# Attention feeding an MLP on one core: three hand-assigned two-bank accumulators, five score jobs at three points, all masks on VectorE, w_out queued ahead of the casts

## The chip, the cores and the metric

One core of one Trainium2 chip. The metric is device time in microseconds (us). A quoted median is over all executions of a kernel in a set of runs; the profile shows one execution, with a *span* a little under its time. Engines: PE is TensorE (matmuls and transposes; PEld are its weight loads), DVE is VectorE, ACT is ScalarE, POOL is GpSimd.

## The reference

Batch 8, 8 heads, 576 positions, 64 dimensions per head. Four heads see a local window of 32 positions, four see every 32nd position. The attention output, 4608 tokens of 512, goes through an MLP with the Mish activation. All inputs and the output are float32.

```python
rel = pos[:, None] - pos[None, :]
mask_local = (rel >= 0) & (rel < 32)
mask_strided = (rel >= 0) & (pos[None, :] % 32 == pos[:, None] % 32)
# heads 0-3 local, heads 4-7 strided; softmax over the allowed positions
attn_out = softmax(where(mask, q @ k.T / 8, -1e9)) @ v
x = attn_out.transpose(0, 2, 1, 3).reshape(4608, 512)
h = x @ w_in                               # 512 -> 2048
out = (h * tanh(softplus(h))) @ w_out      # 2048 -> 512
```

## The kernel before

The MLP runs in nine blocks of 512 tokens. MLP1 of a block is 8 groups of eight matmuls; MLP2 is 16 groups of four. Attention of the next batch is woven in: q and k are transposed between the groups of MLP1, and scores, P times V and the transposes of the result stand between the groups of MLP2. I call P times V of strided tile i "V(s,i)" and of local tile i "V(l,i)". A block takes the time that PE takes for its queue, plus every wait in it.

PSUM is full: three two-bank accumulators (two for the MLP, one for scores) and two one-bank tiles with the tag `pt`. P times V **and** all transposes share these two.

```python
ps_mm = ctx.enter_context(tc.tile_pool(name="psmm", bufs=2, space=PS))
ps_s = ctx.enter_context(tc.tile_pool(name="pss", bufs=1, space=PS))
ps_t = ctx.enter_context(tc.tile_pool(name="pst", bufs=2, space=PS))
...
def tile_t(name):
    return ps_t.tile([128, 512], F32, tag="pt", name=name)
...
def qk(self, kind, i, meng, from_mm=False):      # scores of one job
    ps = tile_s(from_mm)
    ...  # matmuls that contract over 64 rows, half of the array each
    nc.scalar.activation(pt[0:n, :, 0:nw], ps[0:n, :, 0:nw], AF.Exp, scale=scale)
    if meng is not None:
        self.mask(kind, i, meng)                 # P *= mask, on engine meng
...
def pv(self, kind, i):                           # V(kind, i)
    po = tile_t("po")[:, 0:4 * (D + 1)].rearrange("p (h d) -> p h d", h=4)
    self.pv_mm(kind, i, po)
    nc.vector.reciprocal(rden[0:m, :], po[0:m, :, D])       # the normalisation:
    nc.vector.tensor_tensor(...)                            # frees the pt tile
```

Six score jobs per batch, each at its own place in MLP2, four of them masked by GpSimd. Entry i of the list follows group i of MLP2:

```python
Po, Dv = nc.gpsimd, nc.vector
return [
    [Q("s", 0, Dv)], [], [Q("s", 1, Dv)],
    [Q("s", 2, Po), V("s", 0)],
    [Q("l", 0, Po), V("s", 1)],
    [Q("l", 1, Po), V("s", 2), V("s", 3)],
    [Q("l", 2, Po), V("s", 4)], [V("s", 5), V("s", 6)],
    [V("s", 7), V("l", 0)], [V("l", 1)], [X("s", 0), V("l", 2)],
    [X("s", 1), V("l", 3)], [X("l", 0), V("l", 4)], [V("l", 5)],
    [X("l", 1)], [],
]
```

The order of the loads and GpSimd's casts around block 0, where v of batch 1 is first needed:

```python
load_qk_str(1)
load_w_out(0, 2)           # first half of w_out, GpSimd's DMA queue
...
load_v(1)                  # another queue
...
cast_qk_loc(1, Po, Po)
cast_v(1, Po, Po)          # GpSimd waits here until v has landed
load_w_out(2, 4)           # so these are issued only afterwards
load_qk_str(2)
```

The softmax here doesn't subtract the row's maximum and nothing guards it: scores larger than these inputs give would overflow.

Of the kernel before, what the change touches and what calls it, by code (L numbers as in the profile page):

```python
# [16 lines left out]
NW = 6  # L17
WQ = 96
# [19 lines left out]
def kernel(ctx, tc, q, k, v, moe_w_in, moe_w_out, out):  # L38
# [33 lines left out]
    P_s = [const.tile([PN, 2, 6 * PN + 56], BF16, name=f"Ps{i}") for i in range(3)]  # L72
    P_l = [const.tile([128, 2, 4 * WQ + 32], BF16, name=f"Pl{i}") for i in range(3)]
# [9 lines left out]
    ps_mm = ctx.enter_context(tc.tile_pool(name="psmm", bufs=2, space=PS))  # L83
    ps_s = ctx.enter_context(tc.tile_pool(name="pss", bufs=1, space=PS))
    ps_t = ctx.enter_context(tc.tile_pool(name="pst", bufs=2, space=PS))

    def tile_s(from_mm=False):
        if from_mm:
            return ps_mm.tile([128, 2, 512], F32, tag="mm", name="ps")
        return ps_s.tile([128, 2, 512], F32, tag="ps", name="ps")  # L90
# [124 lines left out]
    S_JOBS = [S_UNITS[0:6], S_UNITS[6:12], S_UNITS[12:16]]  # L215
    S_AT = {u: (i, n) for i, job in enumerate(S_JOBS) for n, u in enumerate(job)}

    class Attn:
# [3 lines left out]
        def qk(self, kind, i, meng, from_mm=False):  # L222
            ps = tile_s(from_mm)
            if kind == "l":
                nu, n, w, pt, mk = 4, 128, WQ, P_l[i], loc
                for u in range(nu):
                    hp, c0 = u // 2, WQ * (2 * i + u % 2)
                    for e in range(2):
                        nc.tensor.matmul(  # L229
                            ps[:, e, WQ * u:WQ * u + WQ],  # L230
                            lhsT=kTl[64 * e:64 * e + 64, hp, c0:c0 + 128],
                            rhs=qTl[64 * e:64 * e + 64, hp, c0:c0 + WQ],
                            start=True, stop=True,
                        )
            else:
                nu, n, w, pt, mk = len(S_JOBS[i]), PN, PN, P_s[i], stm
                for u, (jj, h) in enumerate(S_JOBS[i]):
                    c0 = PN * (4 * h + jj)
                    for e in range(2):
                        nc.tensor.matmul(  # L240
                            ps[:, e, PN * u:PN * u + PN],
                            lhsT=kTs[64 * e:64 * e + 64, c0:c0 + 128],
                            rhs=qTs[64 * e:64 * e + 64, c0:c0 + PN],
                            start=True, stop=True,
                        )
            nw = nu * w
            nc.scalar.activation(pt[0:n, :, 0:nw], ps[0:n, :, 0:nw], AF.Exp, scale=scale)  # L247
            if meng is not None:
                self.mask(kind, i, meng)

        def mask(self, kind, i, meng):
            nu, n, w, pt, mk = (
                (4, 128, WQ, P_l[i], loc) if kind == "l" else (len(S_JOBS[i]), PN, PN, P_s[i], stm)
            )
# [7 lines left out]
        def pv_mm(self, kind, i, po):  # L262
            for h in range(4):
                if kind == "l":
                    n, rhs = 128, vl[self.b % 2][:, i, h, :]
                    pt, c0 = P_l[i // 2][:, h % 2], WQ * (2 * (h // 2) + i % 2)
                else:
                    n, rhs = PN, vs[self.b % 2][0:PN, h, i, :]
                    job, u = S_AT[i // 2, h]
                    pt, c0 = P_s[job][:, i % 2], PN * u  # L270
# [17 lines left out]
        def pv2(self, kind, i, from_mm=False):  # L288

            po = tile_s(from_mm)[:, :, 0:4 * (D + 1)].rearrange("p e (h d) -> p e h d", h=4)  # L290
# [38 lines left out]
    def attn_steps(b):  # L329
        a = Attn(b)  # L330
        Po, Dv = nc.gpsimd, nc.vector
# [71 lines left out]
    with tc.manual_schedule():  # L403
# [43 lines left out]
        for i in range(3):  # L447
            a.qk("s", i, None, i > 0)
# [108 lines left out]
```

## Time and profile before

| | before |
|---|---|
| median (range), first three runs | 341.93 us (340.81 to 342.24) |
| span of the profiled execution, mean PE clock | 339.5 us, 0.999 |
| MLP2 of block 0 | 23.11 us (43.11 to 66.22) |
| blocks 1 to 6 (of that, MLP2) | 35.4 to 35.6 us (about 19.5) |

The prediction shows the lines of the page, of the stretches and of PE's timeline. In a line of a timeline the columns are start, length, engine, source line, operation, tiles, shape and number of instructions; a bracket gives the idle time of the engine just before and what ended it. Two rows of the page's list of costly groups are added here. They are P times V, and the columns after the bar are busy us, mean ns of one, idle us of PE just before them in the whole run, and what ended most of it:

```profile
L271 PE MATMUL po<-vs,Ps 72*128 72x65 bf16 x224 | 14.2, 195 | 2.3 <-POOL Ps L256 2.3
...
L271 PE MATMUL po<-vl,Pl 128*128 128x65 bf16 x176 | 12.9, 196 | 2.8 <-DVE rden L282 1.5
```

In 339.5 us PE stands only 5.1 us in front of P times V, and 2.3 of these are the one wait for GpSimd in block 0.

The table of stretches (from:to, length, busy us of PE, PEld, DVE, ACT, POOL, clock, DMA share, GB/s) gives MLP2 of block 0 as

```profile
43.11:66.22 23.11, 19.72 (x221) 10.77 (x223) 11.21 (x34) 10.41 (x13) 14.52 (x14) 1.00 0.82 140
```

### The profile page before, as it was taken

The numbers are of one execution on the slowest core, as the hardware profiler recorded it, in microseconds if no ns is written. First come the engines' busy times: TensorE is split into PE (matmuls) and PEld (weight loads), VectorE is DVE, ScalarE is ACT, GpSimd is POOL, SyncE is SP. The second block draws the span as 40 slices with busy tenths as digits, with TensorE's granted clock in tenths as the row PEclk, the third lists the DMA queues.
The fourth block names the chain that finished last, engine by engine and source line by source line (L and its number), as shares of the span: only waits on it lengthen the run. The fifth ranks groups of instructions, "written<-read, shape, count | busy, mean of one in ns | idle before, by whom it ended". The sixth has DMA issues, their size and how long they took to land.

```text
span 339.5 us, 6425 instructions
## 1 busy us (share of the span) xinstructions
PE 313.8 (92%) x2761; PEld 171.1 (50%) x2808; DVE 114.3 (34%) x306; ACT 176.2 (52%) x194; POOL 111.0 (33%) x105
## 2 busy tenths in 40 slices
PE   2669996999999999999999999999999999999994
PEld 1554553554455545554579555544554454444441
DVE  4670345323552346134622362236323640000000
ACT  3574562556637563747464646564566537414511
POOL 4354049334681049102921094008500700000000
PEclk9999999999999999999999999999999999999999
DMA  6999958999947911595149712941010011011011
GB/s 178 217 220 205 212 95 128 215 200 284 193 110 209 188 37 64 159 198 79 63 116 202 120 62 64 229 74 60 17 51 0 2 64 62 2 62 62 0 57 68
DMA packets 49596, 39.29 MB, mean 116 GB/s; under 512 B 27168, under 2 KB 42080, under 8 KB 49568
## 3 DMA queue, kind: packets, MB, share of 16 engines
q1 hardware_dynamic: 38272, 29.88, 38.6%
q0 software_dynamic: 11152, 8.92, 16.9%
q8 instruction: 22, 0.36, 0.5%
q10 hardware_dynamic: 144, 0.08, 0.1%
q14 instruction: 6, 0.05, 0.1%
HBM read 38.34 MB, written 9.44 MB: 141 GB/s over the span
## 4 chain that ended last, share of the span: by engine, by line
PE 73%; DMA 12%; DVE 4%; POOL 3%; issue 3%; ACT 3%; SPq 1%; POOLq 0%; ACTq 0%
PE psh L368 32%; PE pso L388 28%; DMA vl<-in_v_dram 7%; DMA qs<-in_q_dram 4%; PE po L271 4%; PE tr L174 2%; PE tr L183 2%; ACT Ps L247 2%; DVE x_s L283 1%; PE ps L229 1%; DVE qTl L146 1%; PE ps L240 1%; PE trx L320 1%; PE trx L310 1%; POOL vl L146 1%
## 5 line engine op out<-in xcount | busy, mean ns | idle before, releaser
L388 PE MATMUL pso<-w_out,gT 128*128 128x512 bf16 x546 | 137.3, 379 | 1.6 <-issue 0.2
L368 PE MATMUL psh<-xT,w_in 128*128 128x512 bf16 (+1 forms) x623 | 133.1, 359 | 1.3 <-ACT gT L373 0.2
L373 ACT ACTIVATE gT<-psh 128x1024 bf16<-128x1024 f32 x72 | 73.6, 1024 | 55.7 <-PE psh L368 55.6
L368 PEld LDWEIGHTS <-w_in 128*128 128x128 bf16 x640 | 60.1, 98 | 54.6 <-issue 2.2
L388 PEld LDWEIGHTS <-gT 128*128 128x128 bf16 x576 | 49.0, 97 | 44.3
L144 ACT COPY xT<-trx 128x576 bf16<-128x576 bf16 x32 | 20.3, 639 | 44.1 <-PE trx L320 28.0
L256 POOL TENSOR_TENSOR Ps<-Ps,consts_sb 72x576 bf16<-72x576 bf16 x7 | 8.9, 1273 | 88.8 <-ACT Ps L247 88.7
L256 POOL TENSOR_TENSOR Pl<-Pl,consts_sb 128x768 bf16<-128x768 bf16 x21 | 33.8, 1638 | 1.6 <-ACT Pl L247 1.6
L395 ACT COPY osb<-pso 128x1024 f32<-128x1024 f32 x18 | 18.2, 1012 | 27.4 <-PE pso L388 27.4
L282 DVE RECIPROCAL rden<-po 72x4 f32<-72x4 f32 (+1 forms) x100 | 17.7, 177 | 35.3 <-PE po L271 35.3
L247 ACT ACTIVATE Pl<-ps 128x768 bf16<-128x768 f32 x24 | 19.5, 811 | 14.6 <-PE ps L229 14.4
L283 DVE TENSOR_TENSOR x_s<-po,rden 72x256 bf16<-72x256 f32 x56 | 23.6, 421 | 1.9
L247 ACT ACTIVATE Ps<-ps 72x864 bf16<-72x864 f32 (+1 forms) x24 | 19.1, 806 | 9.5 <-PE ps L240 9.4
L146 DVE COPY kTl<-tr 128x576 bf16<-128x576 bf16 x14 | 10.6, 758 | 30.2 <-PE tr L183 30.2
L146 POOL CAST vs<-vs 72x2048 bf16<-72x2048 f32 x7 | 13.3, 1896 | 18.3 <-DMA vs<-in_v_dram 18.3
L283 DVE TENSOR_TENSOR x_l<-po,rden 96x256 bf16<-96x256 f32 x44 | 18.5, 420 | 1.5
L256 DVE TENSOR_TENSOR Ps<-Ps,consts_sb 72x864 bf16<-72x864 bf16 (+1 forms) x17 | 10.3, 605 | 22.0 <-ACT Ps L247 22.0
L146 DVE COPY kTs<-tr 128x576 bf16<-128x576 bf16 x14 | 6.4, 458 | 30.7 <-PE tr L174 30.7
L271 PEld LDWEIGHTS <-Ps 72*128 72x128 bf16 x256 | 12.1, 102 | 8.8 <-POOL Ps L256 2.4
L271 PE MATMUL po<-vs,Ps 72*128 72x65 bf16 x224 | 14.2, 195 | 2.3 <-POOL Ps L256 2.3
L146 DVE COPY qTl<-tr 128x576 bf16<-128x576 bf16 x14 | 10.6, 756 | 14.8 <-PE tr L183 14.8
L271 PE MATMUL po<-vl,Pl 128*128 128x65 bf16 x176 | 12.9, 196 | 2.8 <-DVE rden L282 1.5
(61 smaller groups left out, 227.0 us busy)
## 6 DMA issues: line engine op xcount, KB each, us to landing
out_dram<-osb SPq DMA_DIRECT2D x18, 512.0 KB, 3.5
vl<-in_v_dram SPq DMA_DIRECT2D x7, 768.0 KB, 17.2
vs<-in_v_dram SPq DMA_DIRECT2D x8, 576.0 KB
kl<-in_k_dram SPq DMA_DIRECT2D x7, 576.0 KB
ql<-in_q_dram SPq DMA_DIRECT2D x7, 576.0 KB, 9.6
w_out<-in_moe_w_out_dram POOLq DMA_DIRECT2D x4, 512.0 KB, 12.5
ks<-in_k_dram POOLq DMA_DIRECT2D x7, 288.0 KB, 12.4
qs<-in_q_dram POOLq DMA_DIRECT2D x7, 288.0 KB, 13.8
```

The costliest lines, as they stand in the source:

```text
L144: nc.scalar.copy(out_, in_)
L146: eng.tensor_copy(out_, in_)
L174: nc.tensor.transpose(tr[:, PN * u:PN * u + PN], src[0:PN, h, 128 * jj:128 * jj + 128], ident[0:PN, 0:PN],)
L247: nc.scalar.activation(pt[0:n, :, 0:nw], ps[0:n, :, 0:nw], AF.Exp, scale=scale)
L256: meng.tensor_tensor(out=pm, in0=pm, in1=mk[0:n, :].unsqueeze(1).unsqueeze(1).to_broadcast([n, 2, nu, w]), op=ALU.mult,)
L271: nc.tensor.matmul(po[:, h, :], lhsT=pt[0:n, c0:c0 + 128], rhs=rhs, start=True, stop=True,)
L282: nc.vector.reciprocal(rden[0:m, :], po[0:m, :, D])
L283: nc.vector.tensor_tensor(out=dst.rearrange("p (h d) -> p h d", h=4), in0=po[0:m, :, 0:D], in1=rden[0:m, :].unsqueeze(2).to_broadcast([m, ...
L368: nc.tensor.matmul(ps[:, u, o:o + n], lhsT=w_in[:, cc, fc * 128:(fc + 1) * 128], rhs=xT[:, cc, a:a + n], start=(cc == 2), stop=(cc == 1),)
L373: nc.scalar.activation(gT[:, 2 * g:2 * g + 2, :], ps[:], AF.Mish)
L388: nc.tensor.matmul(p[:, ot % 2, :], lhsT=gT[:, fc, 128 * ot:128 * ot + 128], rhs=w_out[:, fc, :], start=(fc == 0), stop=(fc == 15),)
L395: nc.scalar.copy(osb[:], p[:])
```

## The change

Its intent: fewer switches of PE between the scores' half-array matmuls and everything else, no wait for a single score accumulator, no slow GpSimd masks, and w_out in time. There are five score jobs at three points of MLP2, each point using accumulators that the MLP leaves free just then; all masks move to VectorE; the second half of w_out and the q/k loads of batch 2 are issued before GpSimd waits for v.

```diff
-    ps_mm = ctx.enter_context(tc.tile_pool(name="psmm", bufs=2, space=PS))
-    ps_s = ctx.enter_context(tc.tile_pool(name="pss", bufs=1, space=PS))
+    ps_a = ctx.enter_context(tc.tile_pool(name="psa", bufs=1, space=PS))
+    def acc(i, name):
+        return ps_a.tile([128, 2, 512], F32, tag=f"acc{i}", name=name)
 ...
+    L_UNITS = [(i, hp) for i in range(NW) for hp in range(2)]
+    PARTS = {
+        "s": [S_UNITS[0:6], S_UNITS[6:12], S_UNITS[12:16]],
+        "l": [L_UNITS[0:5], L_UNITS[5:10], L_UNITS[10:12]],
+    }
 ...
-    def attn_steps(b):
+    def attn_steps(b, x, y):
-        Po, Dv = nc.gpsimd, nc.vector
+        Q = lambda i_acc, *parts: (lambda: a.qk(parts, i_acc, nc.vector))
+        at = [
+            [], [], [],
+            [V("s", 0)], [V("s", 1)], [V("s", 2)], [V("s", 3)], [V("s", 4)],
+            [V("s", 5), V("l", 5)], [V("s", 6), V("l", 0)], [V("s", 7), V("l", 1)],
+            [X("s", 0), V("l", 2)], [X("s", 1), V("l", 3)], [V("l", 4), X("l", 0)], [X("l", 1)], [],
+        ]
+        s0, s1, sl2, l0, l1 = ...
+        if x == y:       # block 0, one accumulator
+            where = {0: [(x, s0)], 2: [(x, s1)], 4: [(x, sl2)], 6: [(x, l0)], 8: [(x, l1)]}
+        else:
+            where = {1: [(x, s0), (y, s1)], 4: [(x, sl2), (y, l0)], 7: [(x, l1)]}
+        for i, jobs in where.items():
+            at[i] = [Q(i_acc, *parts) for i_acc, parts in jobs] + at[i]
 ...
-        load_w_out(0, 2)
+        load_w_out(0, 4)
 ...
         cast_qk_loc(1, Po, Po)
+        load_qk_str(2)
         cast_v(1, Po, Po)
-        load_w_out(2, 4)
-        load_qk_str(2)
```

More of the change, by code (lines that the diff above doesn't have):

```diff
@@ L71 @@
     kTs = const.tile([128, 4 * 4 * PN + 64], BF16, name="kTs")
-    P_s = [const.tile([PN, 2, 6 * PN + 56], BF16, name=f"Ps{i}") for i in range(3)]
-    P_l = [const.tile([128, 2, 4 * WQ + 32], BF16, name=f"Pl{i}") for i in range(3)]
+    P_s = [const.tile([PN, 2, n * PN + 56], BF16, name=f"Ps{i}") for i, n in enumerate((6, 6, 4))]
+    P_l = [const.tile([128, 2, n * WQ + 32], BF16, name=f"Pl{i}") for i, n in enumerate((5, 5, 2))]
     gate = const.tile([1, 256], BF16, name="gate")
@@ L82 @@
     PS = bass.MemoryType.PSUM
-    ps_mm = ctx.enter_context(tc.tile_pool(name="psmm", bufs=2, space=PS))
-    ps_s = ctx.enter_context(tc.tile_pool(name="pss", bufs=1, space=PS))
+    ps_a = ctx.enter_context(tc.tile_pool(name="psa", bufs=1, space=PS))
     ps_t = ctx.enter_context(tc.tile_pool(name="pst", bufs=2, space=PS))
-    def tile_s(from_mm=False):
-        if from_mm:
-            return ps_mm.tile([128, 2, 512], F32, tag="mm", name="ps")
-        return ps_s.tile([128, 2, 512], F32, tag="ps", name="ps")
+    def acc(i, name):
+        return ps_a.tile([128, 2, 512], F32, tag=f"acc{i}", name=name)
     def tile_t(name):
@@ L214 @@
     S_UNITS = [(jj, h) for jj in range(4) for h in range(4)]
-    S_JOBS = [S_UNITS[0:6], S_UNITS[6:12], S_UNITS[12:16]]
-    S_AT = {u: (i, n) for i, job in enumerate(S_JOBS) for n, u in enumerate(job)}
+    L_UNITS = [(i, hp) for i in range(NW) for hp in range(2)]
[3 more added lines that the diff above has]
+    }
+    AT = {kd: {u: (i, n) for i, p in enumerate(PARTS[kd]) for n, u in enumerate(p)} for kd in "sl"}
     class Attn:
@@ L220, in __init__ @@
             self.b = b
-        def qk(self, kind, i, meng, from_mm=False):
-            ps = tile_s(from_mm)
-            if kind == "l":
-                nu, n, w, pt, mk = 4, 128, WQ, P_l[i], loc
-                for u in range(nu):
-                    hp, c0 = u // 2, WQ * (2 * i + u % 2)
-                    for e in range(2):
-                        nc.tensor.matmul(
-                            ps[:, e, WQ * u:WQ * u + WQ],
-                            lhsT=kTl[64 * e:64 * e + 64, hp, c0:c0 + 128],
-                            rhs=qTl[64 * e:64 * e + 64, hp, c0:c0 + WQ],
-                            start=True, stop=True,
-                        )
-            else:
-                nu, n, w, pt, mk = len(S_JOBS[i]), PN, PN, P_s[i], stm
-                for u, (jj, h) in enumerate(S_JOBS[i]):
-                    c0 = PN * (4 * h + jj)
-                    for e in range(2):
-                        nc.tensor.matmul(
-                            ps[:, e, PN * u:PN * u + PN],
-                            lhsT=kTs[64 * e:64 * e + 64, c0:c0 + 128],
-                            rhs=qTs[64 * e:64 * e + 64, c0:c0 + PN],
-                            start=True, stop=True,
-                        )
-            nw = nu * w
-            nc.scalar.activation(pt[0:n, :, 0:nw], ps[0:n, :, 0:nw], AF.Exp, scale=scale)
-            if meng is not None:
-                self.mask(kind, i, meng)
@@ new lines, in qk @@
+        def qk(self, parts, i_acc, meng=None):
+            ps, o = acc(i_acc, "ps"), 0
+            todo = []
+            for kind, i in parts:
+                w = WQ if kind == "l" else PN
+                o0 = o
+                for x, y in PARTS[kind][i]:
+                    for e in range(2):
+                        r = slice(64 * e, 64 * e + 64)
+                        if kind == "l":
+                            lhsT, rhs = kTl[r, y, WQ * x:WQ * x + 128], qTl[r, y, WQ * x:WQ * x + WQ]
+                        else:
+                            c0 = PN * (4 * y + x)
+                            lhsT, rhs = kTs[r, c0:c0 + 128], qTs[r, c0:c0 + PN]
+                        nc.tensor.matmul(ps[:, e, o:o + w], lhsT=lhsT, rhs=rhs, start=True, stop=True)
+                    o += w
+                todo.append((kind, i, o0, o - o0))
+            for kind, i, o0, nw in todo:
+                n, pt = (128, P_l[i]) if kind == "l" else (PN, P_s[i])
+                nc.scalar.activation(pt[0:n, :, 0:nw], ps[0:n, :, o0:o0 + nw], AF.Exp, scale=scale)
+                if meng is not None:
+                    self.mask(kind, i, meng)
@@ L251, in mask @@
         def mask(self, kind, i, meng):
-            nu, n, w, pt, mk = (
-                (4, 128, WQ, P_l[i], loc) if kind == "l" else (len(S_JOBS[i]), PN, PN, P_s[i], stm)
-            )
+            nu = len(PARTS[kind][i])
+            n, w, pt, mk = (128, WQ, P_l[i], loc) if kind == "l" else (PN, PN, P_s[i], stm)
             pm = pt[0:n, :, 0:nu * w].rearrange("p e (u c) -> p e u c", u=nu)
@@ L265, in pv_mm @@
                     n, rhs = 128, vl[self.b % 2][:, i, h, :]
-                    pt, c0 = P_l[i // 2][:, h % 2], WQ * (2 * (h // 2) + i % 2)
+                    part, u = AT["l"][i, h // 2]
+                    pt, c0 = P_l[part][:, h % 2], WQ * u
                 else:
                     n, rhs = PN, vs[self.b % 2][0:PN, h, i, :]
-                    job, u = S_AT[i // 2, h]
-                    pt, c0 = P_s[job][:, i % 2], PN * u
+                    part, u = AT["s"][i // 2, h]
+                    pt, c0 = P_s[part][:, i % 2], PN * u
                 nc.tensor.matmul(
@@ L286, in pv, with pv2 @@
             )
-        def pv2(self, kind, i, from_mm=False):
-            po = tile_s(from_mm)[:, :, 0:4 * (D + 1)].rearrange("p e (h d) -> p e h d", h=4)
+        def pv2(self, kind, i, i_acc):
+            po = acc(i_acc, "po2")[:, :, 0:4 * (D + 1)].rearrange("p e (h d) -> p e h d", h=4)
             m = WQ if kind == "l" else PN
@@ L327, in xt @@
                 )
-    def attn_steps(b):
+    def attn_steps(b, x, y):
         a = Attn(b)
-        Po, Dv = nc.gpsimd, nc.vector
-        Q = lambda kd, i, e: (lambda: a.qk(kd, i, e))
+        Q = lambda i_acc, *parts: (lambda: a.qk(parts, i_acc, nc.vector))
         V = lambda kd, i: (lambda: a.pv(kd, i))
         X = lambda kd, hf: (lambda: a.xt(kd, hf))
-        return [
-            [Q("s", 0, Dv)], [], [Q("s", 1, Dv)],
-            [Q("s", 2, Po), V("s", 0)],
-            [Q("l", 0, Po), V("s", 1)],
-            [Q("l", 1, Po), V("s", 2), V("s", 3)],
-            [Q("l", 2, Po), V("s", 4)], [V("s", 5), V("s", 6)],
-            [V("s", 7), V("l", 0)], [V("l", 1)], [X("s", 0), V("l", 2)],
-            [X("s", 1), V("l", 3)], [X("l", 0), V("l", 4)], [V("l", 5)],
-            [X("l", 1)], [],
-        ]
+        at = [
[3 more added lines that the diff above has]
+            [X("s", 0), V("l", 2)], [X("s", 1), V("l", 3)], [V("l", 4), X("l", 0)], [X("l", 1)], [],
+        ]
+        s0, s1, sl2, l0, l1 = (("s", 0),), (("s", 1),), (("s", 2), ("l", 2)), (("l", 0),), (("l", 1),)
+        if x == y:
+            where = {0: [(x, s0)], 2: [(x, s1)], 4: [(x, sl2)], 6: [(x, l0)], 8: [(x, l1)]}
+        else:
+            where = {1: [(x, s0), (y, s1)], 4: [(x, sl2), (y, l0)], 7: [(x, l1)]}
+        for i, jobs in where.items():
+            at[i] = [Q(i_acc, *parts) for i_acc, parts in jobs] + at[i]
+        return at
     def segs(t):
@@ L353, in segs, with mlp1 @@
         return r
-    def mlp1(t):
+    def mlp1(t, accs):
         gT = g_pool.tile([128, 16, 512], BF16, tag="gT", name="gT")
@@ L361, in group @@
             if g not in held:
-                held[g] = ps_mm.tile([128, 2, 512], F32, tag="mm", name="psh")
+                held[g] = acc(accs[g % 3], "psh")
             ps = held[g]
@@ L378, in mlp1, with mlp2 @@
         return gT, [lambda g=g: group(g) for g in range(8)]
-    def mlp2(t, gT, fc_major=False):
+    def mlp2(t, gT, accs, fc_major=False):
         po = {}
@@ L384, in group @@
             if ot // 2 not in po:
-                po[ot // 2] = ps_mm.tile([128, 2, 512], F32, tag="mm", name="pso")
+                po[ot // 2] = acc(accs[ot // 2], "pso")
             p = po[ot // 2]
@@ L447 @@
         for i in range(3):
-            a.qk("s", i, None, i > 0)
+            a.qk([("s", i)], i)
         a.mask("s", 0, Dv)
@@ L460 @@
             t_step_loc0(kl0, kTl[:, hp, 32:32 + S], hp, Sc)
-        a.pv2("s", 0)
+        a.pv2("s", 0, 0)
         a.mask("s", 2, Dv)
-        a.pv2("s", 2, True)
+        a.pv2("s", 2, 1)
         for hp in range(2):
             t_step_loc0(ql0, qTl[:, hp, :], hp, Sc)
-        a.qk("l", 0, None, True)
-        a.pv2("s", 4)
-        a.qk("l", 1, None, True)
+        a.qk([("l", 0)], 2)
+        a.pv2("s", 4, 0)
+        a.qk([("l", 1)], 1)
         a.mask("l", 0, Dv)
-        a.pv2("s", 6)
+        a.pv2("s", 6, 0)
         cast_v_loc(0, Sc, 3, 6)
-        a.qk("l", 2, None, True)
+        a.qk([("l", 2)], 2)
         a.mask("l", 1, Dv)
         load_qk_str(1)
-        load_w_out(0, 2)
+        load_w_out(0, 4)
         nc.sync.dma_start(gate[:], qs[1][0:1, 0, 0:256])
         load_v(1)
-        gT, g1 = mlp1(0)
+        accs = (2, 1, 0)
+        gT, g1 = mlp1(0, accs)
         a.xt("s", 0)
@@ L481 @@
         Sc.preload_act_table(AF.Mish)
-        a.pv2("l", 0, True)
+        a.pv2("l", 0, 1)
         a.mask("l", 2, Dv)
-        a.pv2("l", 2)
+        a.pv2("l", 2, 0)
         a.pv("l", 4)
@@ L499 @@
         for t in range(NBLK):
+            x, y, z = accs
             if t > 0:
-                gT, g1 = mlp1(t)
-            ts = t_steps(t + 1) if t + 1 < B else []
-            at = attn_steps(t + 1) if t + 1 < B else []
+                gT, g1 = mlp1(t, accs)
+            ts, at = [], []
             if t == 0:
+                ts, at = t_steps(1), attn_steps(1, y, y)
                 at[8].append(load_next)
                 at[0] = ts[2:4] + at[0] + [lambda: load_qk_str(3)]
+                out_accs, accs = (z, x), (y, z, x)
+            else:
+                if t + 1 < B:
+                    ts, at = t_steps(t + 1), attn_steps(t + 1, x, y)
+                out_accs, accs = (z, y), (z, x, y)
             for i, g in enumerate(g1):
@@ L515 @@
                 load_qk_str(t + 3)
-            for i, g in enumerate(mlp2(t, gT, fc_major=(t == 0))):
+            for i, g in enumerate(mlp2(t, gT, out_accs, fc_major=(t == 0))):
                 g()
```

## The prediction

> **What bounds the kernel now.** I read the page's busy shares first, then the table of stretches, then TensorE's timeline in one block, and then the same microseconds on the engines that feed it. The page:
>
> ```profile
> PE 313.8 (92%) x2761; PEld 171.1 (50%) x2808; DVE 114.3 (34%) x306; ACT 176.2 (52%) x194; POOL 111.0 (33%) x105
> ```
>
> TensorE (PE) is the bound on average. By stretches (columns: from:to, length, then busy us of PE, PEld, DVE, ACT, POOL, then clock, DMA share, GB/s):
>
> ```profile
> 58.60:102.00 43.40, 42.66 (x395) 22.68 (x400) 17.80 (x51) 23.76 (x27) 23.54 (x20) 1.00 1.03 200
> 137.40:172.80 35.40, 34.61 (x320) 18.38 (x325) 14.12 (x38) 20.19 (x22) 14.04 (x12) 1.00 0.60 120
> 307.00:334.80 27.80, 27.55 (x126) 12.37 (x127) 0.00 (x0) 10.22 (x11) 0.00 (x0) 1.00 0.10 38
> ```
>
> A block (512 tokens, MLP1 then MLP2) with the attention of the next batch woven in takes 35.4 us; the last two, without attention, take 27.8. Blocks 1 to 6 are alike, block 0 has a start of its own. So the change must be judged by what TensorE waits for in such a block. Its timeline around the scores of a batch (start, length, instructions; a group of four MLP2 matmuls is L388, the scores L240 and L229, P times V L271):
>
> ```profile
> 153.11 1.03 PE L388 MATMUL pso<-w_out,gT 128*128 128x512 bf16 x4
> 154.08 0.37 PE L240 MATMUL ps<-qTs,kTs 64*128 64x72 bf16 x12
> 154.38 1.68 PE L388 MATMUL pso<-w_out,gT 128*128 128x512 bf16 x7
> 156.33 0.37 PE L240 MATMUL ps<-qTs,kTs 64*128 64x72 bf16 x12 [0.27 <-ACT Ps L247]
> 156.64 1.04 PE L388 MATMUL pso<-w_out,gT 128*128 128x512 bf16 x4
> ...
> 163.39 1.03 PE L388 MATMUL pso<-w_out,gT 128*128 128x512 bf16 x4
> 164.26 0.29 PE L271 MATMUL po<-vs,Ps 72*128 72x65 bf16 x4
> 164.79 0.29 PE L271 MATMUL po<-vl,Pl 128*128 128x65 bf16 x4 [0.25 <-DVE rden L282]
> 164.92 1.02 PE L388 MATMUL pso<-w_out,gT 128*128 128x512 bf16 x4
> ```
>
> A group occupies 4 x 0.216 = 0.86 us (eight MLP1 matmuls take 1.73 on the chain that ended last). The reader is to see two kinds of loss: about 0.11 us before each score job (153.11 + 0.86 = 153.97, scores at 154.08) and 0.12 after it, six times a batch; and two real waits, one for the single score accumulator (0.12 us beyond the usual 0.11) and one of 0.25 for a small PSUM buffer that VectorE (DVE) had not emptied. Feeding engines:
>
> ```profile
> 158.08 0.65 ACT L247 ACTIVATE Ps<-ps 72x576 bf16<-72x576 f32 x1 [0.45 <-PE ps L240]
> 159.46 0.81 ACT L247 ACTIVATE Pl<-ps 128x768 bf16<-128x768 f32 x1 [0.73 <-PE ps L229]
> 163.39 1.01 ACT L395 COPY osb<-pso 128x1024 f32<-128x1024 f32 x1 [0.26 <-PE pso L388]
> ```
>
> ```profile
> 157.66 0.60 DVE L256 TENSOR_TENSOR Ps<-Ps,consts_sb 72x864 bf16<-72x864 bf16 x1 [0.74 <-ACT Ps L247]
> 158.25 0.18 DVE L282 RECIPROCAL rden<-po 72x4 f32<-72x4 f32 x1
> 158.46 0.42 DVE L283 TENSOR_TENSOR x_s<-po,rden 72x256 bf16<-72x256 f32 x1
> ```
>
> One normalisation on DVE (reciprocal and multiply) is 0.63 us. In block 0 alone GpSimd (POOL) holds PE up:
>
> ```profile
> 56.76 0.29 PE L271 MATMUL po<-vs,Ps 72*128 72x65 bf16 x4 [2.27 <-POOL Ps L256]
> ```
>
> **What the Trainium skill says.** (1) "TensorEngine Tiling (Array Packing)", Key Properties: "Mode switching requires drain". The scores contract over 64 rows, all else uses the whole array; the 0.11 + 0.12 us at each score job agree. (2) "TensorE: Matmul & The Clock Gate", Architectural detail: ScalarE and VectorE queues are strict FIFO; only weight loads are pulled ahead on TensorE. The timelines agree so far as they show: no DVE instruction is out of program order. My prediction rests on this. (3) "PSUM — Partial Sum Buffer", Specifications: 8 banks of 512 fp32. Three two-bank accumulators plus two one-bank tiles fill all eight, before and after: P times V and the transposes still share only two small tiles. (4) "SBUF — State Buffer", Who interferes with whom: a VectorE instruction with two SBUF inputs contends with GpSimd reads. In block 0 a mask took 0.76 instead of 0.60 us beside a POOL cast, so this is small.
>
> **The change part by part.**
> *Fewer switches.* Blocks 1 to 6 have three score points instead of six. Matmul work is equal. 3 x 0.23 = 0.69 us saved per block. With scores in alternating accumulators the 0.12 us wait goes too.
> *Masks on DVE.* POOL loses 1.27 + 4.83 = 6.1 us per batch, none of it on the path in blocks 1 to 6. DVE gains four masks: 0.45 (four strided units, 446 ns in the prologue), two of five local units, one of two. The local one of 768 columns took 0.545; with the slope between 576 and 864 columns, (614 - 446)/288 = 0.58 ns, I estimate 0.66, 0.66, 0.32. In sum 2.1 us; DVE rises from 14.1 to 16.2 of 35.4 and stays idle on average. But the instruction order shows the new masks standing in DVE's queue ahead of normalisations whose PSUM tile PE wants back: mask s2, l2, l0, then the normalisation of V(s,1); and mask l1 ahead of that of V(s,4), while exp l1 itself stands behind the output copy on ScalarE (ACT).
> *Walk through one MLP2*, times in us from its start, group 0.86, P times V 0.13, exp of 960 columns 0.97 (slope (886 - 647)/288 = 0.83 ns).
> - Second point, PE at 5.05: first score at 5.16, exp s2 from 5.55 (first score to exp 0.40 as at 157.68 and 158.08 before), then exps 0.65, 0.49, 0.97, overlapping 0.1 each as in the prologue (0.89 + 0.89 + 0.65 took 2.20): exp l0 ends 7.4. Mask l0 to 8.1, normalisation of V(s,1) to 8.65. PE does V(s,1), group 5, V(s,2), group 6 and needs that tile for V(s,3) at 7.65. **Stall 1.0 to 1.1.**
> - Third point, PE at 9.7: output copy 9.95 to 10.95, exp l1 to 11.8, mask l1 to 12.5, normalisation of V(s,4) to 13.05. PE does l1 scores, V(s,4), group 8, V(s,5) and wants the tile for V(l,5) at 11.2. **Stall 1.9.**
> - Groups 8, 9 and 10 carry two P times V each: two normalisations need 2 x 0.55 at their back-to-back pitch, against 0.86 + 0.26 on PE, with DVE already late: **0.3** more, in place of the old 0.25.
>
> The same addition for the kernel before gives 19.34 us for its MLP2; measured 153.11 to 172.65 is 19.54. For the changed one it gives 21.49. So +2.15 per block: gains 0.69 + about 0.1 + 0.25, losses 3.2. Times six blocks: **+12.9 us**.
> *Block 0.* One accumulator is used five times. No POOL masks, so the 2.27 and 0.30 us waits go. Walking it the same way there are DVE stalls of 0.4, 0.8 and 0.4 (V(l,5), V(s,6), V(l,0)); its MLP2 becomes 21.7 against 23.1 (43.11 to 66.22): -1.4.
> *w_out ahead of the casts.* No PE wait for w_out shows now, so nothing is gained directly. About 8 us of transfers (two w_out pieces and two q/k loads: 1600 packets of some 82 ns over 16 engines, from the queue's 16.9% share and 11152 packets) now compete with the load of v of batch 1, which landed at 48.8. I estimate it 4 us later, cast done near 55, needed near 54.7: +0.3.
> *Start.* Third accumulator in MLP1 of block 0: the 0.25 us wait for ACT goes. Shorter last local mask: -0.2.
>
> Sum: 341.9 + 12.9 - 1.4 + 0.3 - 0.25 - 0.2 = **353.2 us**.
>
> **Rivals.** (a) *The gain comes through*: DVE is idle 60% of the time and no tile is late. Then -1.05 x 6 - 1.4 - 0.15 gives about 334 us. For it: the averages. Against it: the order of DVE's queue and two small tiles, which the averages hide. (b) *Half of the stalls*: should exps, masks or hand-overs be 0.3 us quicker than added up, the stalls shrink to about 2.2 us and the time to about 347. Against: all durations are measured. (c) *v arrives late in block 0*: if w_out takes the larger share of the DMA, V(s,0) and V(l,5) wait 3 to 5 us there: about 357. For it: DMA is 90% busy up to 42 us; against: only 50% in the slice in which v landed. (d) *POOL casts now meet DVE's masks*: 0.15 us each, below 1 us per block.
>
> **Range and chances.** An error of 0.5 us in the stalls of a block is 3 us in all, block 0 adds 1.5 either way: 348.5 to 357.5. Slower by over 2% (above 348.8) 0.87, within 2% 0.09, faster 0.04 (rival a).
>
> **What would show it.** In MLP2 of blocks 1 to 6: PE waiting near 1 us for DVE before V(s,3) and near 2 us before V(l,5); three score points, small gaps beside each; blocks of 37.5 us; PE busy time unchanged but its share down to 89%; the normalisation after a mask starting long after its matmul. In block 0: no wait for POOL, gap of 2.27 gone. The prediction is wrong if DVE runs these normalisations before the masks, if the tiles do not rotate over two buffers, or if v of batch 1 holds PE up for microseconds.

## The result, and the profile after

| | before | after |
|---|---|---|
| median (range), 4 runs each | 341.37 us (340.19 to 342.24) | 357.75 us (356.27 to 358.75) |
| span and clock of the profiled execution | 339.5 us, 0.999 | 356.4 us, 0.988 |
| MLP2 of block 0 | 23.11 us | 25.87 us |
| block 1 | 35.56 us | 38.38 us |
| blocks 2 to 6 | 35.4 to 35.6 us | 37.58 to 37.74 us |

The ratio is 1.048 (95% interval 1.043 to 1.053): 4.8% slower. A ratio here is the mean time of one kernel's fast runs over that of the other's fast runs of the same rounds, so it is not quite the ratio of the medians. The time is 4.6 us above the predicted one and 0.25 us above the top of its range. So the direction was foreseen, and something was missing in the sum.

The page after, its row of busy shares and its rows for P times V:

```profile
PE 313.8 (88%) x2763; PEld 171.7 (48%) x2808; DVE 128.2 (36%) x334; ACT 173.3 (49%) x194; POOL 69.7 (20%) x77
...
L268 PE MATMUL po<-vl,Pl 128*128 128x65 bf16 x192 | 14.4, 204 | 15.4 <-DVE rden L279 10.9
...
L268 PE MATMUL po<-vs,Ps 72*128 72x65 bf16 x256 | 18.8, 203 | 6.6 <-DVE x_s L280 5.8
```

PE is busy for the same 313.8 us. The idle time in front of P times V rose from 5.1 to 22.0 us. GpSimd was relieved of 41 us that had cost almost nothing, and DVE took over 14, which brought it to only 36%; yet DVE is what now ends PE's waits. The stretches (block 0's MLP2, blocks 1 and 2):

```profile
43.83:69.70 25.87, 21.92 (x222) 11.70 (x223) 13.95 (x38) 10.16 (x13) 8.36 (x8) 0.87 0.91 173
69.70:108.08 38.38, 34.45 (x320) 18.18 (x325) 16.55 (x42) 19.76 (x22) 12.22 (x12) 1.00 0.70 147
108.08:145.66 37.58, 34.26 (x320) 18.27 (x325) 15.80 (x42) 19.76 (x22) 8.04 (x8) 1.00 0.52 113
```

Block 2 has PE busy for 34.3 of 37.6 us. MLP2 of block 0 has a mean clock of 0.87; in the kernel before, every such stretch had 1.00. So there are two things to explain.

PE's timeline in block 2:

```profile
125.80 0.56 PE L239 MATMUL ps<-qTs,kTs 64*128 64x72 bf16 x24
126.52 1.67 PE L389 MATMUL pso<-w_out,gT 128*128 128x512 bf16 x7 [0.16 <-issue]
...
129.65 0.30 PE L268 MATMUL po<-vs,Ps 72*128 72x65 bf16 x4
...
132.72 0.30 PE L268 MATMUL po<-vs,Ps 72*128 72x65 bf16 x4 [0.92 <-DVE x_s L280]
133.81 0.39 PE L239 MATMUL ps<-qTl,kTl 64*128 64x96 bf16 x10
...
137.23 0.29 PE L268 MATMUL po<-vl,Pl 128*128 128x65 bf16 x4 [1.81 <-DVE rden L279]
```

Both predicted stalls are there: 0.92 us in front of V(s,3) and 1.81 in front of V(l,5) (predicted 1.0 to 1.1, and 1.9). The three score points cost 0.60, 0.64 and 0.42 us beside the MLP's groups, 1.66 in sum against 2.48 for the six before, so the saving is real too. Why DVE is late stands in its own timeline of the same block:

```profile
130.22 0.59 DVE L252 TENSOR_TENSOR Ps<-Ps,consts_sb 72x576 bf16<-72x576 bf16 x1 [1.12 <-ACT Ps L244]
130.74 0.34 DVE L252 TENSOR_TENSOR Pl<-Pl,consts_sb 128x384 bf16<-128x384 bf16 x1
131.46 0.66 DVE L252 TENSOR_TENSOR Pl<-Pl,consts_sb 128x960 bf16<-128x960 bf16 x1 [0.38 <-ACT Pl L244]
132.03 0.17 DVE L279 RECIPROCAL rden<-po 72x4 f32<-72x4 f32 x1
...
135.88 0.66 DVE L252 TENSOR_TENSOR Pl<-Pl,consts_sb 128x960 bf16<-128x960 bf16 x1 [2.13 <-ACT Pl L244]
136.46 0.17 DVE L279 RECIPROCAL rden<-po 72x4 f32<-72x4 f32 x1
```

The P times V at 129.65 is done before 130. Its normalisation starts at 132.03, behind three masks, and the last of these had to wait for an exponential on ScalarE. DVE was idle in that time, for the last 0.27 of the 1.12 us and for the 0.38, with the normalisation ready to run behind an instruction that was not. Lower down it idled 2.13 us for one mask, the last 1.46 of them with the normalisation of V(s,4) ready behind it.

In block 0 PE's timeline shows another wait:

```profile
58.88 0.38 PE L268 MATMUL po<-vl,Pl 128*128 128x65 bf16 x4 [2.99 <-POOL vl L144]
...
61.22 1.90 PE L389 MATMUL pso<-w_out,gT 128*128 128x512 bf16 x4
```

V(l,5) waited 2.99 us for v of batch 1, and a group of MLP2 then took 1.90 us in place of the usual 1.03. A stretch of two microseconds shows the granted clock (the third number from the end):

```profile
60.00:62.00 2.00, 2.00 (x13) 0.95 (x12) 0.71 (x4) 0.00 (x0) 0.44 (x1) 0.50 0.90 252
```

GpSimd's first cast of local v starts when the load has landed. Before, then after:

```profile
48.77 1.24 POOL L146 CAST vl<-vl 128x768 bf16<-128x768 f32 x1 [1.89 <-DMA vl<-in_v_dram]
```

```profile
56.89 1.94 POOL L144 CAST vl<-vl 128x768 bf16<-128x768 f32 x2 [8.02 <-DMA vl<-in_v_dram]
```

v landed 8.1 us later.

### The profile page after: what moved, and what is told of

Read it like the earlier page. It is cut to its first block, busy times and chain, and to the rows that moved or that the text cites. A ratio compares the mean times of both kernels' runs of the same rounds, so it can differ in the third digit from the quotient of the medians.

```text
span 356.4 us, 6406 instructions
## 1 busy us (share of the span) xinstructions
PE 313.8 (88%) x2763; PEld 171.7 (48%) x2808; DVE 128.2 (36%) x334; ACT 173.3 (49%) x194; POOL 69.7 (20%) x77
## 5 line engine op out<-in xcount | busy, mean ns | idle before, releaser
L389 PEld LDWEIGHTS <-gT 128*128 128x128 bf16 x576 | 50.1, 98 | 46.3 <-issue 1.6
L142 ACT COPY xT<-trx 128x576 bf16<-128x576 bf16 x32 | 20.2, 640 | 54.7 <-PE trx L317 45.6
L268 PE MATMUL po<-vl,Pl 128*128 128x65 bf16 x192 | 14.4, 204 | 15.4 <-DVE rden L279 10.9
L252 DVE TENSOR_TENSOR Ps<-Ps,consts_sb 72x864 bf16<-72x864 bf16 (+1 forms) x24 | 16.4, 686 | 24.5 <-ACT Ps L244 24.3
L268 PE MATMUL po<-vs,Ps 72*128 72x65 bf16 x256 | 18.8, 203 | 6.6 <-DVE x_s L280 5.8
L268 PEld LDWEIGHTS <-Ps 72*128 72x128 bf16 x256 | 14.7, 103 | 20.6 <-DVE x_s L280 10.1
L279 DVE RECIPROCAL rden<-po 96x4 f32<-96x4 f32 (+1 forms) x100 | 17.4, 174 | 16.7 <-PE po L268 16.7
L244 ACT ACTIVATE Pl<-ps 128x960 bf16<-128x960 f32 (+1 forms) x24 | 18.7, 806 | 3.6 <-PE ps L239 3.5
L252 DVE TENSOR_TENSOR Pl<-Pl,consts_sb 128x960 bf16<-128x960 bf16 (+1 forms) x24 | 13.6, 568 | 16.8 <-ACT Pl L244 16.7
L144 POOL CAST vl<-vl 128x768 bf16<-128x768 f32 x15 | 13.2, 904 | 31.8 <-DMA vl<-in_v_dram 31.8
L268 PEld LDWEIGHTS <-Pl 128*128 128x128 bf16 x192 | 10.3, 104 | 18.6 <-issue 14.1
```

Of the source, the lines that this page charges most:

```text
L142: nc.scalar.copy(out_, in_)
L144: eng.tensor_copy(out_, in_)
L244: nc.scalar.activation(pt[0:n, :, 0:nw], ps[0:n, :, o0:o0 + nw], AF.Exp, scale=scale)
L252: meng.tensor_tensor(out=pm, in0=pm, in1=mk[0:n, :].unsqueeze(1).unsqueeze(1).to_broadcast([n, 2, nu, w]), op=ALU.mult,)
L268: nc.tensor.matmul(po[:, h, :], lhsT=pt[0:n, c0:c0 + 128], rhs=rhs, start=True, stop=True,)
L389: nc.tensor.matmul(p[:, ot % 2, :], lhsT=gT[:, fc, 128 * ot:128 * ot + 128], rhs=w_out[:, fc, :], start=(fc == 0), stop=(fc == 15),)
```

## The experiments

**Theory A:** in blocks 1 to 6 the loss is a matter of order. Masks that are not ready stand in DVE's queue ahead of normalisations, and the two `pt` tiles let PE run no further. **Theory B:** in block 0 the loss is v, delayed by the loads that are now queued ahead of it; its wait also costs clock. **Rival C:** VectorE is simply too slow for all the masks, so that no order helps. **Rival D:** the new accumulators, or the larger score jobs, are at fault. All kernels here gave correct results. Kernels of one chip share their runs of the kernel before: chip 12 had e1 to e4 (before 340.24 us), chip 11 had e1b and e5 to e7 (340.00), chip 13 had e8 and the two combined kernels (340.26).

### Block 0: what delays v

**e1_wout_late.** From the changed kernel, only w_out's second half goes back behind the casts.

```diff
-        load_w_out(0, 4)
+        load_w_out(0, 2)
 ...
         load_qk_str(2)
         cast_v(1, Po, Po)
+        load_w_out(2, 4)
```

> The changed kernel with one part undone: the third and fourth w_out transfers are queued behind the casts again; the q/k loads of batch 2 stay ahead of the v casts. Theory A (v of batch 1 is delayed by the whole time of what is queued ahead of it, w_out about 5.2 us of the 8.2 us added): v lands near 51.5 us instead of 56.9, its cast ends near 53.6, before it is needed at 55.7; the 2.99 us wait for it and the stretch of lowered clock after it both go, DVE stalls of 1.6 us in sum show in their place, MLP2 of block 0 takes about 21.7 us instead of 25.9, total about 353.6. Rival B (the wait comes from the q/k loads or from POOL's own order, not from w_out): v still lands near 56.9, total unchanged at 357.8.

Measured: 363.28 us, ratio 1.064 (1.057 to 1.071). The execution that was profiled took 828 us, with 512-column matmuls of some 800 ns, while the other three took 359.6 to 364.1. I do not know what disturbed it, and its page is not used.

**e1b_wout_late.** The same kernel, one execution with a profile.

> The same kernel as e1, for a profile of an ordinary execution (that of e1 was of an execution of 828 us). By what the run with both parts late showed: v lands near 51, no wait for v; instead the w_out pieces land after they are needed, a wait for w_out of 3 to 6 us before group 8 of block 0 and a lowered clock after it; 360 to 364 us.

Measured: 363.23 us (a single run, state unknown), clock 0.983. v landed at 52.65, 4.2 us earlier than in the changed kernel, but MLP2 of block 0 grew to 28.71 us, because PE then stood for w_out:

```profile
60.75 1.86 PE L389 MATMUL pso<-w_out,gT 128*128 128x512 bf16 x4 [4.77 <-DMA w_out<-in_moe_w_out_dram]
```

What follows: w_out *does* matter in block 0. In the kernel before, PE's 2.27 us wait for a GpSimd mask ended at 56.76, just after the third piece of w_out had landed (56.64). In the changed kernel that wait is gone, PE comes for this piece earlier, and it is on the path.

**e2_qk_late.** From the changed kernel, only the q/k loads of batch 2 go back behind the cast.

```diff
         cast_qk_loc(1, Po, Po)
-        load_qk_str(2)
         cast_v(1, Po, Po)
+        load_qk_str(2)
```

> The changed kernel with only the q/k loads of batch 2 put back behind the v casts; w_out stays ahead. Theory A: their transfers are about 3 us of the 8.2 us added, v lands near 54, cast done near 56, so that P times V of the local half waits 0 to 0.5 us, too short to lower the clock; total about 353.8. Rival (only w_out matters): v lands near 56.9, total 357.8. Rival B (only the q/k loads matter): v lands near 48.8.

Measured: 355.04 us, ratio 1.042 (1.039 to 1.046), so 2.7 us below the changed kernel's median. MLP2 of block 0 took 22.72 us with the clock at 1.0 throughout. GpSimd's timeline:

```profile
54.33 2.02 POOL L144 CAST vl<-vl 128x768 bf16<-128x768 f32 x2 [4.93 <-DMA vl<-in_v_dram]
```

v came 2.6 us earlier; PE waited only 0.72 us for it (for the strided half, in front of V(s,0)), and 0.55, 0.34 and 0.34 us for DVE. Between these two profiled executions block 0's MLP2 shrank by 3.15 us (25.87 to 22.72). The direction is surer than the size: all four times of e2 (354.03 to 355.64) lie below all four of the changed kernel, but the intervals of the two ratios overlap a little, and e5 below shows how much block 0 varies.

**e3_both_late.** Both go back.

```diff
-        load_w_out(0, 4)
+        load_w_out(0, 2)
 ...
-        load_qk_str(2)
         cast_v(1, Po, Po)
+        load_w_out(2, 4)
+        load_qk_str(2)
```

> The changed kernel with the transfer order of before (both parts back). Theory A: v lands near 48.8 as before; MLP2 of block 0 about 21.7 us, with DVE stalls of about 0.4, 0.8, 0.4; total 353.5, that is the predicted 353.2 within a microsecond; blocks 1 to 6 unchanged at 37.6. If block 0 stays at 25 us the cause lies in its accumulators and not in the transfers.

Measured: 357.31 us, ratio 1.049 (1.043 to 1.056): no gain over the changed kernel. v landed at 48.44, as early as in the kernel before. But PE waited 2.92 us for w_out, its clock fell to 0.57 and the next group took 1.87 us; MLP2 of block 0 was 25.96 us. The expectation had put such a block 0 down to the accumulators; the wait names w_out instead, and e2 has the same accumulators with 22.72 us.

What follows from the three together: v lands at 48.4 with nothing queued ahead, at 54.3 with w_out (5.9 later), at 52.7 with the q/k loads (4.2 later) and at 56.9 with both (8.5 later). Executions of other kernels with the same orders agree: v landed at 47.8 to 48.8 us with nothing ahead (before, e3, e7), at 53.5 to 54.3 with w_out (e2 and the two combined kernels), at 55.5 to 57.1 with both (the changed kernel, e4, e5, e6, e8). So theory B holds as to what delays v. The best of the four orders is e2's: w_out early, q/k late.

**e8_before_wout.** The other direction: the kernel *before*, with only the reordering of loads added.

```diff
-        load_w_out(0, 2)
+        load_w_out(0, 4)
 ...
         cast_qk_loc(1, Po, Po)
+        load_qk_str(2)
         cast_v(1, Po, Po)
-        load_w_out(2, 4)
-        load_qk_str(2)
```

> The kernel before with the transfer part of the change alone: all four w_out pieces and the q/k loads of batch 2 queued ahead of the v casts; old accumulators, score jobs and GpSimd masks. Theory: v of batch 1 lands near 57 us as in the changed kernel, the GpSimd masks stand behind its cast and two transfers, so that P times V of strided group 6 waits until about 62 us, some 7 us instead of 2.27, and TensorE's clock drops after it; 347 to 349. Rival (w_out queued ahead is harmless or helpful by itself): 338 to 340.

Measured: 347.22 us, ratio 1.019 (1.014 to 1.025), inside the 347 to 349 expected. v landed at 56.30. MLP2 of block 0 took 27.58 us against 23.11, the other blocks' MLP2 19.54 as before.

```profile
60.94 0.40 PE L271 MATMUL po<-vs,Ps 72*128 72x65 bf16 x4 [5.22 <-POOL Ps L256]
```

The wait is for GpSimd's mask, which stands in its queue behind the cast that waits for v. The clock was 0.50 to 0.57 from 58 to 64 us. The reordering alone thus costs some 7 us (347.22 against 340.26), with no other part of the change present; the ratio is clear of 1.

### Blocks 1 to 6: order or throughput

**e4_v_first.** From the changed kernel, P times V of a place goes ahead of the scores of that place, so that its normalisation is queued ahead of their masks. Same work, same engines.

```diff
-            at[i] = [Q(i_acc, *parts) for i_acc, parts in jobs] + at[i]
+            at[i] = at[i] + [Q(i_acc, *parts) for i_acc, parts in jobs]
```

> The changed kernel with P times V put ahead of the scores within a step, so that each normalisation enters DVE's queue before the masks of that step. Work on every engine is the same. Theory (head of DVE's in-order queue): the stalls of 0.92 before V(s,3) and 1.81 before V(l,5) shrink to about 0.2 and 0.7, with 0.4 before V(s,6): MLP2 of blocks 1 to 6 takes 19.95 us instead of 21.69, total 357.8 - 10.4 = 347.4. Rival (DVE has too much work in this stretch, in whatever order): nothing changes, 357.8.

Measured: 345.57 us, ratio 1.015 (1.012 to 1.019), below the 347.4 expected. MLP2 of a steady block is 19.88 us (expected 19.95) in place of 21.69. In PE's timeline the stalls in front of V(s,3) and V(l,5) are gone, and two short ones stand in front of V(s,6) and V(l,0):

```profile
132.93 0.30 PE L268 MATMUL po<-vs,Ps 72*128 72x65 bf16 x4 [0.50 <-DVE x_s L280]
...
133.56 0.29 PE L268 MATMUL po<-vl,Pl 128*128 128x65 bf16 x4 [0.34 <-DVE rden L279]
```

DVE does exactly as much as in the changed kernel, and most of the loss in these blocks is gone. Rival C falls, and rival D with it, since accumulators and jobs are untouched.

**e6_l1_early.** From the changed kernel, the last score job comes one group earlier, so that its exponential is not behind the output copy on ScalarE.

```diff
-            where = {1: [(x, s0), (y, s1)], 4: [(x, sl2), (y, l0)], 7: [(x, l1)]}
+            where = {1: [(x, s0), (y, s1)], 4: [(x, sl2), (y, l0)], 6: [(x, l1)]}
```

> The changed kernel with the third score job (l1) one group earlier in blocks 1 to 6, so that its exp is queued ahead of the output copy on ScalarE; masks stay on VectorE and ahead of the normalisations of their step. Theory: the stall before V(s,3) takes its place in the queue as before (0.6 after the score job instead of 0.9), the chain copy - exp - mask - normalisation loses the copy's 1.0 us and starts a group earlier, so that the 1.81 before V(l,5) falls to about 0.2; MLP2 19.6 us, total 345.2. Rival (it is the order within DVE's queue alone, the copy plays no part): the stall before V(l,5) falls by less than 1 us and the total stays above 350.

Measured: 343.92 us, ratio 1.013 (1.009 to 1.017); MLP2 19.55 (expected 19.6), which alone is 2.1 us per block. The stall in front of V(l,5) is gone and the other shrank:

```profile
128.70 0.29 PE L268 MATMUL po<-vs,Ps 72*128 72x65 bf16 x4 [0.60 <-DVE x_s L280]
```

Only the place of one job was moved, so it is shown that the late mask of this job made the stall. How much of that is the output copy and how much the start one group earlier is not separated.

**e5_pool_l.** From the changed kernel, the two large local masks of blocks 1 to 6 go back to GpSimd; DVE's queue keeps only short masks.

```diff
+                    pool = kind == "l" and i < 2 and self.b > 1
-                    self.mask(kind, i, meng)
+                    self.mask(kind, i, nc.gpsimd if pool else meng)
```

> The changed kernel with the two long local masks (l0, l1) of batches 2 to 7 on GpSimd instead of VectorE; all else as changed. Theory (masks at the head of DVE's queue hold back the normalisations): both stalls of 0.92 and 1.81 us go although exp l1 still stands behind the output copy; in their place some 0.3 before V(l,0) and 0.2 before V(l,2); MLP2 of blocks 1 to 6 18.96 us instead of 21.69, total 357.8 - 16.4 = 341.4, block 0 unchanged at 25.9. Rival (the stall before V(l,5) comes from the late exp l1, whoever masks): that stall stays at about 1.8 and the total is about 351.

Measured: 337.77 us, ratio 0.993 (0.990 to 0.997), better than the 341.4 expected. MLP2 is 18.89 us (expected 18.96) and a block 34.78. The masks are three times slower on GpSimd, and PE hardly notices. The last exponential still stands behind the output copy here, and the stall in front of V(l,5) is gone all the same; so a late exponential does harm only where its mask stands in DVE's queue. GpSimd's line, then PE's largest remaining stall, in front of V(l,0):

```profile
124.23 1.99 POOL L253 TENSOR_TENSOR Pl<-Pl,consts_sb 128x960 bf16<-128x960 bf16 x1 [14.30 <-ACT Pl L244]
```

```profile
128.40 0.29 PE L269 MATMUL po<-vl,Pl 128*128 128x65 bf16 x4 [0.24 <-DVE rden L280]
```

The rest of the surprise is block 0, whose program is that of the changed kernel: in this execution v landed at 55.50, V(l,5) waited only 1.63 us for it, the clock did not fall, and MLP2 took 22.45 us in place of 25.87. The same program took 25.68 us there in e4 and 25.40 in e6, with waits of 2.96 and 2.99. So block 0 of the changed order varies by some 3 us from execution to execution.

**e7_before_dve.** The kernel *before*, with only the masks moved to VectorE: six jobs at six points, the old accumulators, the old loads.

```diff
-        Po, Dv = nc.gpsimd, nc.vector
+        Po = Dv = nc.vector
```

> The kernel before with one part of the change alone: its four GpSimd masks per batch go to VectorE, in the old six score jobs. Theory: the masks stand ahead of normalisations of the same step, stalls of about 0.6 and 0.9 us before the third and fifth P times V of the strided half; MLP2 of blocks 1 to 6 20.8 us instead of 19.5, in block 0 the GpSimd wait goes and a wait for w_out of up to 2 us shows; total 340.2 + 7.3 - 0.5 = 347. Rival (the masks cost nothing by themselves, only the batching of the scores makes them late): 338 to 340.

Measured: 351.06 us, ratio 1.030 (1.025 to 1.036), above the 347 expected. In steady blocks MLP2 is 20.80 us, exactly as expected, with stalls of about 0.45 and 0.83 us. The wait for w_out in block 0 that was expected did not come: its third piece landed at 55.79 and was first used at 57.41. Most of the miss is in block 1 (39.43 us against 36.70 in the later ones), where one mask met a cast on GpSimd that began at 92.22 and lasted 1.89 us. VectorE's line:

```profile
92.82 1.70 DVE L256 TENSOR_TENSOR Pl<-Pl,consts_sb 128x768 bf16<-128x768 bf16 x1 [0.46 <-ACT Pl L247]
```

The same mask took 0.56 us elsewhere. PE then stalled 1.97 us, and its clock was 0.50 from 96.2 to 99.6. What follows: moving the masks is enough to lose over a microsecond a block; rival D is refuted a second time. And item (4) of the prediction, contention with GpSimd, is not always small: here the mask, begun 0.60 us after the cast, lasted until after the cast's end.

### The parts that pay, together

**b_pool.** The edits of e2, e4 and e5 on the changed kernel.

> A version meant to beat both: the changed kernel with the q/k loads of batch 2 back behind the v casts, P times V ahead of the scores within a step, and the two long local masks of batches 2 to 7 on GpSimd. Theory: MLP2 of blocks 1 to 6 18.9 us as with the GpSimd masks alone, block 0 about 22 us without a wait for v and without a lowered clock; 336.5, against 340.2 before. If the switch of transfers costs elsewhere (q/k of batch 2 late for their transposes), a wait shows in MLP1 of block 1.

Measured (5 rounds): 336.32 us (335.23 to 336.71), ratio 0.987 (0.983 to 0.991), expected 336.5. MLP2 of block 0 and block 1 in the stretches:

```profile
44.10:65.60 21.50, 19.94 (x226) 11.09 (x223) 12.78 (x38) 10.16 (x13) 6.54 (x8) 1.00 0.79 140
65.60:100.40 34.80, 34.54 (x326) 18.63 (x325) 14.69 (x40) 19.74 (x22) 18.06 (x15) 1.00 0.99 197
```

PE is busy for 34.54 of 34.80 us and the clock is full. Against the kernel before, a block is some 0.6 us shorter, close to the 0.69 that the prediction worked out for three fewer score points. It is 1.3% faster than the kernel before and 6% faster than the changed one; the interval excludes 1.

**b_dve.** The edits of e2, e4 and e6: all masks stay on VectorE, only orders differ.

> The same with all masks left on VectorE and the third score job one group earlier instead: only order is changed against the changed kernel, no work moves between engines. Theory: MLP2 of blocks 1 to 6 19.1 to 19.2 us (one stall of about 0.4 and one of 0.3), block 0 about 22; 338, a little below before. Rival (VectorE's load of 16.2 us per block is too much in any order): no better than 343.

Measured: 339.28 us, ratio 0.996 (0.991 to 1.001); expected 338. MLP2 is 19.09 us in steady blocks, 19.97 in block 1. So order alone wins back all that the change lost. The masks on VectorE still give nothing over those on GpSimd.

## Why the prediction was right or wrong

The spans of the two profiled executions differ by 16.9 us; the prediction's parts add up to 11.35.

| part | predicted | measured |
|---|---|---|
| blocks 1 to 6 | +12.9 | +13.6 (2.82 in block 1, 10.74 in 2 to 6) |
| MLP2 of block 0, with v | -1.1 | +2.8 |
| start, up to block 0's MLP2 | -0.45 | +0.7 |
| the last two blocks and the end | 0 | -0.15 |

**Walk through one MLP2: right.** 21.49 us was added up, 21.68 to 21.69 measured in blocks 2 to 6; with the sum's own shortfall for the kernel before (19.34 for 19.54) taken off, the difference of 2.15 us is exact. This is not luck of the sum: counted from start to start of PE's instructions, the three losses are 1.08, 1.97 and 0.32 us (the brackets give 0.92, 1.81 and 0.16, as they begin at the modelled end of the matmul before). Both stalls, their places and their causes are those predicted, and e4 and e6 remove or shrink them by order alone. Rivals (a), that the gain comes through, and (b), that the stalls are half as large, did not come about.

**Fewer switches: right.** 1.66 us for three points against 2.48 for six is 0.8 us a batch; b_pool shows the gain once nothing hides it.

**w_out ahead of the casts: this step failed.** It said "I estimate it 4 us later, cast done near 55, needed near 54.7: +0.3". v came 8.1 us later: by all of the estimated 8 us of transfers, and not by half. SyncE issued the load of local v only 0.46 us later than before (38.40 against 37.94), so nearly all of the delay arose while it was being served. The DMA view of the changed kernel from 42.0 to 55.3 us gives (GpSimd's queue, then v's; packets, MB, share of 16 engines):

```profile
q0 software_dynamic: 1562, 1.34, 60.3%
q1 hardware_dynamic: 3247, 1.26, 48.2%
```

So v was not held back until the rest was done; the two moved about equal amounts side by side, and v landed at 56.89, 1.6 us after the last of the others (55.30). This is where the halving went wrong: even if engines that are busy all the time are shared evenly, the load that lands last is late by all the work that was done before it.

Of the 25.87 us of MLP2 in block 0, e2 shows what is left without that wait: 22.72 less its own 0.72 for v is 22.0, near the 21.7 that the walk gave. So the term of +0.3 measured about +3.9 in this execution. Up to V(l,5) the changed kernel was 1.27 us behind e2 (15.05 against 13.78), and from there to the end of that MLP2 1.88 us more (10.82 against 8.94; e5, with the same program as the changed kernel there, 8.86). With e2's own 0.72, about 2.0 of the 3.9 us are thus the wait, as far as it does not stand in place of waits for VectorE, and about 1.9 come after it, while the clock was down. Rival (c) had named this wait and its size, and 357 us; it was given too small a share of the predicted time. Had the term been 3.9, the sum would have been 356.8. In e5's execution it was about 0.45 (22.45 less 22.0), close to the predicted 0.3, so the size of this term is partly a matter of when v happens to land.

That the clock falls because PE idles is a reading of several executions, not an experiment of its own, and no length of wait separates the cases. In block 0 it fell to about half after waits of 2.92 us and more (2.92 in e3, 2.96 in e4, 2.99 in the changed kernel and e6, 4.77 in e1b, 5.22 in e8), and it stayed at 1.0 after 1.63 in e5 and 2.27 in the kernel before. But it also fell after the 1.97 of e7, and in e2 and e1b after one of the waits of 1.81 us in front of V(l,5), which left it at 1.0 in other blocks. e2's stretch:

```profile
172.20:175.50 3.30, 3.21 (x15) 1.50 (x15) 2.09 (x8) 0.00 (x0) 0.00 (x0) 0.50 0.00 0
```

The MLP2 in which it lies took 23.09 us, those of the blocks before and after it 21.68 and 21.67.

**"No PE wait for w_out shows now, so nothing is gained directly": incomplete.** It did not ask what would become of w_out once the GpSimd wait in front of it was gone. e3 and e1b show 2.92 and 4.77 us of PE waiting for w_out. So with the rest of the change this part was needed; only the q/k loads, moved along with it, were not (e2).

**Rival (d), masks against casts: under-sized where it strikes.** Block 1 of the changed kernel took 0.8 us more than the next ones, with its masks beside GpSimd casts, which is still below the 1 us of (d); e7 shows 1.70 us for a mask of 0.56. The prediction had called this small from one mask of 0.76 us. That mask began at 46.57, when the cast beside it had only 0.31 us left to run, so it could not show the full size.

**Start.** +0.7 in place of -0.45. Over all executions profiled (e1's disturbed one left out), with nearly the same program up to that point, MLP2 of block 0 began between 43.0 and 44.5 us, so I take this for variation between executions and claim no cause.

**What stays open.** Why v moved so little at first (0.09 MB against 0.69 on GpSimd's queue from 38.4 to 42.0 us), and why block 0 varies so much between executions. What sets the moment at which the clock falls. What disturbed the 828 us execution. Whether a third `pt` tile would make the order of masks harmless: PSUM is full, so it could not be tried without another design.

## What to carry to other kernels

An engine that is 36% busy can still set the time: what counts is which instruction stands ahead in its queue and how many buffers let the others run on while it waits for its input. Put the instruction that frees a scarce buffer ahead of the one whose input is not ready yet, or give the latter to an idle engine even at three times its duration. When transfers are moved forward, or a wait is removed, look for the load that had just been in time, and sum what now lies ahead of it at its full length.

## What the Trainium skill lacked or had wrong

- "DMA: Bandwidth & Descriptors", Queues, rings and completion order: each engine alternates between the queues that it has work for, packet by packet. The 1.34 and 1.26 MB that the two queues moved from 42.0 to 55.3 us fit this; the 0.69 and 0.09 MB of the 3.6 us before do not show it. The page gives no example of how much two loads of different queues delay each other: here v came 8.1 us later behind an estimated 8.2 us of transfers, and in the experiments 5.9 (w_out), 4.2 (q/k) and 8.5 us (both).
- "TensorE: Matmul & The Clock Gate", Why this matters for your kernels: no idle gaps above about 3 us between matmuls. These runs agree only in part: half clock after every wait of 2.92 us and more, none after 2.27 in the kernel before, but half clock for about 3.4 us also after 1.97 in e7 and after one wait of 1.81 in e2 and one in e1b.
- "TensorEngine Tiling (Array Packing)", Key Properties: the drain at a change of mode has no figure. Here the two sides of a score point cost about 0.11 and 0.12 us.
